# Three reorderings in a fused attention and two-layer MLP kernel: when a bank is copied out, through which buffers layer 1's sums leave, and when layer 2 begins

## The chip, the cores and the metric

The kernel runs on one core of one Trainium2 chip. The metric is the device time of one execution in microseconds (us). A run of the kernel gives one time; the profiler's trace comes from one further execution, which has a time of its own. The engines are TensorE (PE, with its weight loads listed as PEld), VectorE (DVE), ScalarE (ACT), GpSimd (POOL) and SyncE (SP, which here only issues DMAs). Each runs its own instructions strictly in the order in which they stand, and they meet through semaphores.

## What the reference computes

```python
# attention: 4 batches, 8 heads, 576 positions, head_dim 64
q_d, k_d, v_d = (t.reshape(B, H, 144, 4, D).mean(axis=3) for t in (q, k, v))
out_d = softmax(q_d @ k_d.T / 8) @ v_d                 # coarse: on means of 4 positions
local = softmax(where(|i - j| < 4, q @ k.T / 8, -1e9)) @ v
x = (repeat(out_d, 4) + local) as (2304, 512)          # 2304 tokens
# layer 1 (moe_w_in 512x2048, moe_w_out 2048x512)
h = x @ w_in; y = (h * sigmoid(1.702 * h)) @ w_out
# layer 2, the same weights again: g = h if h > 0 else exp(h) - 1
h2 = y @ w_in; out = elu(h2) @ w_out
```

The weights reach the kernel as 64-bit numbers and are converted on the chip, for each layer anew.

## The kernel before, in words

**Precision.** A float32 operand is split into a high and a low part (names ending in `h` and `l`); each product is the sum of three matmuls, high x high, low x high and high x low. So one step of 512 tokens (12 matmuls for four chunks of 128) costs the same on the way in (`h`) and out (`y` in layer 1, `o` in layer 2).

**Layer 1** goes over blocks of tokens (two of 256 that are later handled as one, `both`, then 512, 512, 512 and 256). For a block it takes the 2048 hidden columns in 16 steps `f`: 12 matmuls into a bank of PSUM (`h_part`), tanh on ACT (`h_tanh`), the gate on DVE (`h_gate`, which is what empties the bank), the high part on ACT (`h_high`) and the low part on DVE (`h_low`). Two steps later the result is multiplied with the outgoing weights into four banks `y` that stay open over the whole block (`y_part`). After the last step ACT copies the four banks to SBUF tiles `ye` (the line with `scale=0.5`), and SP writes them to a DRAM buffer, `ydram`. There are two banks for `h`; step f + 2 needs the bank of step f.

**Attention** of the later units (a unit is a batch and two heads) is interleaved with layer 1 in pieces: two matmul groups `qk` and `qkd` (local and coarse scores), exponentials on ACT, weights on DVE, transposes `pdt` and `ptr`, and the products with v, `pvd` and `pv`. Their results become x of a later block. All their PSUM tiles take turns in two banks of one pool (`spool`). In `turned_over` five transposes go out: four into one bank (`ptr0`), the fifth into the first columns of another (`ptr1`); DVE copies the first bank, ACT the second; then the coarse product goes into the remaining columns of the second bank. There are eight such units.

**Layer 2** reads `ydram` back (`load_y`), splits it (`split_y`: `x2h` on ACT, `x2l` on DVE) and runs the same scheme in `products_h2` and `products_o2`. Its weights are converted while layer 1's last block and layer 2's first block run: for each of 32 weight tiles ACT makes two passes (`ww2i`, `ww2o`, then `whl2i`, `whl2o`), DVE four. The conversion tiles `ww` of layer 1 lie in a pool `stage1`, three buffers deep.

**Order.** PE's order in this part is that of the code (`step1` writes it out). ACT, DVE and SP are ordered by a scheduler from the program order, the data and the buffers, with its own costs, so a change of buffers moves instructions there too. The lines that matter: `pt` and `turned_over`; in `y_part` the choice of the tile for `ye` (tag `g` of `gpool`, two buffers, which the gate's tiles use as well); in `step1` the call of `hidden2` for layer 2's steps 0 and 1, while layer 1's last two products are still to come.

Of the kernel before, what the change touches and what calls it, by code (L numbers as in the profile page):

```python
# [8 lines left out]
F32 = mybir.dt.float32  # L9
# [6 lines left out]
AF = mybir.ActivationFunctionType  # L16
# [3 lines left out]
P = 128  # L20
# [7 lines left out]
NK = 4  # L28
# [95 lines left out]
NPAIR = len(WINDOWS) // 2  # L124
# [9 lines left out]
def kernel(  # L134
# [20 lines left out]
    nc = tc.nc  # L155
# [3 lines left out]
    NBLK = len(BLOCKS1)  # L159
# [14 lines left out]
    for half in range(2):  # L174
        rows = slice(64 * half, 64 * half + 64)
        for a, e, lo in ((0, 1, -3), (1, 5, 0), (5, 6, 3)):
            m = mask[rows, a:e, :]
            for step, base, mult in ((1, -lo, -1), (-1, lo + 6, 1)):
                nc.gpsimd.affine_select(
                    out=m, in_=m, pattern=[[0, e - a], [step, KW]], compare_op=ALU.is_ge, fill=NEG,  # L180
# [182 lines left out]
    l1a = ExitStack()  # L363
# [46 lines left out]
    class Unit:  # L410
# [264 lines left out]
        def sums(self):  # L675
            return sumset[:, units.index(self) % NSUM]
# [45 lines left out]
        def pt(self, a, e):  # L722
            self.pt_copy(a, e, self.pt_piece(a, e))
# [204 lines left out]
    class Packed(Unit):  # L928
# [64 lines left out]
        def pt(self):  # L993
            while not self.weighed:
                deferred.pop(0)()
            self.PT = self.t([P, NPAIR, P], "PT")
            ps = self.ps([P, NPAIR - 1, P], "ptr0"), self.ps([P, P + SD], "ptr1")
            for i in range(NPAIR):
                nc.tensor.transpose(
                    out=ps[0][:, i] if i < NPAIR - 1 else ps[1][:, :P],  # L1000
                    in_=self.sl[:, 2 * i:2 * i + 2].rearrange("p s k -> p (s k)"), identity=ident,
                )
            nc.vector.tensor_copy(out=self.PT[:, :NPAIR - 1], in_=ps[0])
            nc.scalar.activation(out=self.PT[:, NPAIR - 1], in_=ps[1][:, :P], func=AF.Copy)
            return ps[1][:, P:]

        def pv_down_products(self, ps):
            for kc in range(2):
# [5 lines left out]
            return ps  # L1014

        def turned_over(self):
            ps = self.pt()
            self.pv_down_copy(self.pv_down_products(ps))

        def pv_products(self):  # L1020
            ps = [self.ps([P, 87, 4], f"pv{i}") for i in range(2)]
# [54 lines left out]
    queue = [(rest[NREST].turn, None, 1)]  # L1076
# [12 lines left out]
    nsplit = [0]  # L1089
# [118 lines left out]
    def sums_of(blk):  # L1208

        at = BOTH if blk in (0, 1) else blk  # L1210
        n = 512 if at == BOTH else BLOCKS1[at][1]
        if at not in yps:
            yps[at] = [
                ypool.tile([P, 512], F32, tag=f"y{i % 2}", name=f"y{i}_{at}") for i in range(NK * n // 512)
            ]
        first = 256 if blk == 1 else 0
        size = 512 if blk == BOTH else BLOCKS1[blk][1]
        per = 512 // n

        def sums(m):  # L1220
            at0 = first + n * (m % per)
            return yps[at][m // per][:, at0:at0 + size]

        return yps[at], per, sums

    def y_part(blk, fs, half):
        banks, per, sums = sums_of(blk)
        gh, gl = hg[blk, fs]
        opens = fs[0] == 0 and blk != 1
        last = fs[-1] == NF - 1  # L1230
        for m in (2 * half, 2 * half + 1):
            n = 0
            for i, f in enumerate(fs):
                for wp, gp in ((0, gh), (0, gl), (1, gh)):
                    nc.tensor.matmul(  # L1235
                        out=sums(m), lhsT=w_out(1, f, wp)[:, m, :], rhs=gp[:, i, :],
                        start=(opens and n == 0 and m % per == 0), stop=(last and n == 3 * len(fs) - 1),
                        skip_group_check=True,
                    )
                    n += 1  # L1240
            if last and m % per == per - 1:
                t0, tb = (0, 512) if blk == BOTH else BLOCKS1[blk]
                if blk == NBLK - 1:
                    t = x2pools[0].tile([P, 512], F32, tag="y32", name=f"ye{m // per}_{blk}", bufs=2)
                else:
                    t = gpool.tile([P, 512], F32, tag="g", name=f"ye{m // per}_{blk}", bufs=2)
                nc.scalar.activation(out=t, in_=banks[m // per], func=AF.Copy, scale=0.5)  # L1247
                nc.sync.dma_start(
                    out=ydram[m - per + 1:m + 1, :, t0:t0 + tb].rearrange("c p t -> p c t"),
                    in_=t.rearrange("p (a b) -> p a b", a=per),  # L1250
                )
        if half == 1:
            del hg[blk, fs]
# [11 lines left out]
    stage1 = ls1.enter_context(tc.tile_pool(name="stage1", bufs=1, side="right"))  # L1265
# [4 lines left out]
    wt1 = Weights(1, order1, stage1, 3, lambda tag: True, NSIGN)  # L1270
# [3 lines left out]
    kd, f = spare.pop(0)  # L1274
# [9 lines left out]
    steps = [(blk, fs) for blk in (0, 1) for fs in pairs[:FIRST]] + [(BOTH, (f,)) for f in range(2 * FIRST, NF)]  # L1284
# [94 lines left out]
    def hidden2(s):  # L1379
        bi, f = steps2[s]  # L1380
        wt2.need("i", f)
        low_part = products_h2(s)
        if bi + 1 < len(blocks):
            if 8 <= f < 8 + NK:
                load_y(bi + 1, f - 8)
            if 10 <= f < 10 + NK:
                split_y(bi + 1, f - 10)
        wt2.load(AHEAD + wt2.half - wt2.loaded)
        with behind():
            wt2.convert()  # L1390
        low_part()
        if s % 4 == 3:
            with behind():
                wt2.convert()
# [38 lines left out]
    def step1(si, blk, fs):  # L1433
        nonlocal prev, wt2, stage1, stage2, l1a, wextra, used
        chunks = []
        if blk is not None:
            last_blk = 1 if blk == BOTH else blk
            while not ready(last_blk):
                assert attend()
            if last_blk > 1 and fs[0] == 0:  # L1440

                with behind_step(si):
                    for _ in range(NK):
                        split_some(blk)
                while waiting:
                    prev = waiting.pop(0)
                    wt1.need("o", prev[1][-1])
                    chunks.append(products_y1(*prev))
            while nsplit[0] < NK * (last_blk + 1):
                split_some(last_blk)  # L1450
            wt1.need("i", fs[-1])
            chunks.append(products_h1(blk, fs))
            waiting.append((blk, fs))
            if blk == NBLK - 1:
                used |= {f"wi{f}" for f in fs}
        if len(waiting) > LAG or blk is None:
            prev = waiting.pop(0)
            wt1.need("o", prev[1][-1])
            chunks.append(products_y1(*prev))
        if blk is None:  # L1460
            hidden2(si - len(steps))
        nchunk = 0
        for chunk in chunks:
            for _ in chunk:
                if not wt1.finished() and (blk == 0 or si < 3 * FIRST and si % 2 == 1):
                    wt1.convert()
                with behind_step(si):
                    attend()
                if blk == 0:
                    split_some(1)  # L1470
                nchunk += 1
                if wt2 is not None and nchunk in (2, 3) and (nchunk == 2 or si % 2):
                    wt2.load(AHEAD + wt2.half - wt2.loaded)
                    with behind():
                        wt2.convert()
        if blk == NBLK - 1:
            f2 = fs[0] // 2
            if 1 <= f2 <= NK:
                load_y(0, f2 - 1)
            if 3 <= f2 < 3 + NK:  # L1480
                split_y(0, f2 - 3)
        if chunks and prev is not None and prev[0] == NBLK - 1:
            used |= {f"wo{f}" for f in prev[1]}
        if wt1.finished() and stage1 is not None:
            ls1.close()
            stage1 = None
        if not queue and nsplit[0] == NK * NBLK and l1a is not None:
            l1a.close()
            l1x.close()
            l1s.close()  # L1490
            hpools.append(ls2.enter_context(tc.tile_pool(name="hpool2", bufs=2, space=PSUM, side="right")))
            l1a = None
            stage2 = ls2.enter_context(tc.tile_pool(name="stage2", bufs=1, side="right"))
            x2pools.append(ls2.enter_context(tc.tile_pool(name="x2a", bufs=1, side="right")))
            wextra = ls2.enter_context(tc.tile_pool(name="wextra", bufs=1, side="right"))
            for i, tile2 in enumerate(order2):
                places[(2, *tile2)] = (wextra, f"we{i}") if i < NEXTRA else (wpool, released[i - NEXTRA])
            used |= {f"we{i}" for i in range(NEXTRA)}
            wt2 = Weights(2, order2, stage2, 3, lambda tag: tag in used, 0)
            wt2.load(AHEAD)  # L1500
# [14 lines left out]
    for s in range(LAG, len(steps2) + LAG):  # L1515
        if s < len(steps2):
            hidden2(s)
        f = steps2[s - LAG][1]
# [34 lines left out]
```

## Time and profile before

| | |
|---|---|
| median of 3 runs | 948.66 us (946.81 to 949.02) |
| the profiled execution, its own time | 949.08 us |
| its span (first to last instruction) | 947.3 us |
| PE busy | 921.0 us, 97% |
| DVE busy, ACT busy, POOL busy | 502.3 us, 465.4 us, 78.9 us |
| mean granted clock of TensorE | 0.998 |

The stretches, in us from the span's start: attention with layer 1's first blocks until about 180; layer 1's block 2 from there to about 303; block 3 to about 406; block 4 to about 494; the 256-token block 5 to about 546; layer 2 from about 535 to the end. PE's matmuls are pipelined, and their ends are modelled; what counts is where PE stands idle, and what ended each of these waits.

### The profile page before, as it was taken

How to read it: one execution, taken by the hardware profiler on the slowest of the kernel's cores; microseconds unless marked ns; L12 is line 12 of the kernel's file. 1: busy time of each engine (PE TensorE's matmuls, PEld its weight loads, DVE VectorE, ACT ScalarE, POOL GpSimd, SP SyncE). 2: the span in 40 equal slices, each digit the busy share in tenths (PEclk: the TensorE clock that was granted, in tenths of full speed). 3: DMA queues.
4: the chain of work that ended last, by engine and by line, in shares of the span. 5: the costliest groups of instructions: out<-in, count | busy, mean ns of one | idle time of the engine just before them, and what ended most of it. 6: DMA issues, size and time to landing. Idle time of an engine off the chain costs nothing. (4 is left out here: it accounts for less than half of the span.)

```text
span 947.3 us, 14840 instructions
## 1 busy us (share of the span) xinstructions
PE 921.0 (97%) x5812; PEld 756.0 (80%) x5812; DVE 502.3 (53%) x920; ACT 465.4 (49%) x1131; POOL 78.9 (8%) x126
## 2 busy tenths in 40 slices
PE   8998999989999899999999989999999999999998
PEld 5687888767777678888889978877888888888897
DVE  6999987665665542322227898773224222322232
ACT  6879997454353532232235576653334333433343
POOL 3615114101111100000000000000000000000000
PEclk9999999999999999999999999999999999999999
DMA  9897803333332104010029620011002000100010
GB/s 186 185 254 227 226 21 67 87 66 62 64 62 70 45 15 134 0 45 1 1 69 351 248 80 9 1 45 45 0 1 79 1 1 0 56 1 1 1 45 23
DMA packets 113590, 68.04 MB, mean 72 GB/s; under 512 B 81008, under 2 KB 103024, under 8 KB 113520
## 3 DMA queue, kind: packets, MB, share of 16 engines
q1 hardware_dynamic: 111152, 66.50, 25.9%
q8 instruction: 46, 0.75, 0.4%
q10 hardware_dynamic: 2368, 0.59, 0.4%
q14 instruction: 24, 0.20, 0.1%
HBM read 57.63 MB, written 9.44 MB: 71 GB/s over the span
## 5 line engine op out<-in xcount | busy, mean ns | idle before, releaser
L1407 PE MATMUL o<-whl2o,g2h 128*128 128x512 f32 x576 | 181.3, 395 | 3.1 <-ACT ye L1247 2.8
L1358 PE MATMUL h<-x2h,whl2i 128*128 128x512 f32 (+1 forms) x640 | 159.0, 370 | 0.0
L1235 PE MATMUL y<-g1h,whl1o 128*128 128x512 f32 (+1 forms) x512 | 153.5, 367 | 0.0
L1168 PE MATMUL h<-xh,whl1i 128*128 128x512 f32 (+1 forms) x640 | 145.1, 351 | 2.7 <-DVE g L1181 2.7
L1368 DVE SCALAR_TENSOR_TENSOR g<-e,h 128x512 f32<-128x512 f32 (+1 forms) x80 | 50.7, 634 | 177.9 <-ACT e L1366 177.6
L1358 PEld LDWEIGHTS h<-x2h,whl2i 128*128 128x128 f32 x640 | 114.3, 188 | 22.4
L1407 PEld LDWEIGHTS o<-whl2o,g2h 128*128 128x128 f32 x576 | 107.5, 189 | 27.9 <-ACT ye L1247 3.2
L1365 ACT ACTIVATE e<-h 128x512 f32<-128x512 f32 (+1 forms) x80 | 44.3, 554 | 159.5 <-PE h L1358 159.5
L1168 PEld LDWEIGHTS h<-xh,whl1i 128*128 128x128 f32 x640 | 106.1, 189 | 20.3 <-DVE g L1181 3.5
L1407 PE MATMUL o<-whl2o,g2l 128*128 128x512 f32 x288 | 113.0, 392 | 0.0
L1181 DVE SCALAR_TENSOR_TENSOR g<-g,h 128x512 f32<-128x512 f32 x64 | 43.9, 686 | 122.1 <-ACT g L1177 122.1
L1235 PEld LDWEIGHTS y<-g1h,whl1o 128*128 128x128 f32 x512 | 92.6, 189 | 16.7 <-issue 1.4
L1177 ACT ACTIVATE g<-h 128x512 f32<-128x512 f32 x64 | 38.1, 595 | 123.1 <-PE h L1168 118.2
L1235 PE MATMUL y<-g1l,whl1o 128*128 128x512 f32 (+1 forms) x256 | 93.0, 363 | 0.0
L1358 PE MATMUL h<-x2l,whl2i 128*128 128x512 f32 (+1 forms) x320 | 79.6, 370 | 0.0
L1168 PE MATMUL h<-xl,whl1i 128*128 128x512 f32 (+1 forms) x320 | 75.9, 351 | 0.0
L1375 DVE TENSOR_TENSOR g2l<-g,g2h 128x512 fp32r<-128x512 f32 (+1 forms) x80 | 51.6, 646 | 36.8 <-ACT g2h L1373 21.6
L1373 ACT ACTIVATE g2h<-g 128x512 fp32r<-128x512 f32 (+1 forms) x80 | 47.1, 589 | 42.8 <-DVE g L1368 42.7
L1358 PEld LDWEIGHTS h<-x2l,whl2i 128*128 128x128 f32 x320 | 56.7, 188 | 11.0
L1407 PEld LDWEIGHTS o<-whl2o,g2l 128*128 128x128 f32 x288 | 54.5, 189 | 12.1
L1168 PEld LDWEIGHTS h<-xl,whl1i 128*128 128x128 f32 x320 | 53.3, 189 | 8.5 <-issue 0.8
L1194 DVE TENSOR_TENSOR g1l<-g,g1h 128x512 fp32r<-128x512 f32 x64 | 44.4, 693 | 25.4 <-ACT g1h L1187 25.1
(142 smaller groups left out, 1289.6 us busy)
## 6 DMA issues: line engine op xcount, KB each, us to landing
wst1i<-in_moe_w_in_dram SPq DMA_DIRECT2D x16, 512.0 KB
wst1o<-in_moe_w_out_dram SPq DMA_DIRECT2D x16, 512.0 KB
wst2i<-in_moe_w_in_dram SPq DMA_DIRECT2D x16, 512.0 KB
wst2o<-in_moe_w_out_dram SPq DMA_DIRECT2D x16, 512.0 KB
vr<-in_v_dram SPq DMA_DIRECT2D x32, 144.0 KB
out_dram<-ot SPq DMA_DIRECT2D x18, 256.0 KB
y<-ydram SPq DMA_DIRECT2D x16, 256.0 KB
ydram<-ye SPq DMA_DIRECT2D x14, 256.0 KB
```

The lines of the kernel that those rows point to most:

```text
L1168: nc.tensor.matmul(out=hps[blk, fs][:, i, :], lhsT=w_in(1, f, c, wp), rhs=columns(xp, c), start=(n == 0), stop=(n >= len(todo) - nf), skip ...
L1177: return nc.scalar.activation(out=g, in_=hps[blk, fs], func=AF.Tanh, scale=0.851)
L1181: return nc.vector.scalar_tensor_tensor(out=g, in0=g, scalar=1.0, in1=ph, op0=ALU.add, op1=ALU.mult)
L1194: return nc.vector.tensor_tensor(out=gl, in0=g, in1=gh.bitcast(F32), op=ALU.subtract)
L1235: nc.tensor.matmul(out=sums(m), lhsT=w_out(1, f, wp)[:, m, :], rhs=gp[:, i, :], start=(opens and n == 0 and m % per == 0), stop=(last and ...
L1358: nc.tensor.matmul(out=ph[:, :n], lhsT=w_in(2, f, c, wp), rhs=xp[:, c, :n], start=(i == 0), stop=(i == 3 * NK - 1),)
L1365: nc.scalar.activation(out=e[:, :n], in_=ph[:, :n], func=AF.Relu, scale=-1.0)
L1368: urgent["dve"] = nc.vector.scalar_tensor_tensor(out=g[:, :n], in0=e[:, :n], scalar=-1.0, in1=ph[:, :n], op0=ALU.add, op1=ALU.max)
L1373: nc.scalar.activation(out=gh[:, :n], in_=g[:, :n], func=AF.Copy)
L1375: return lambda: nc.vector.tensor_tensor(out=gl[:, :n], in0=g[:, :n], in1=gh[:, :n].bitcast(F32), op=ALU.subtract)
L1407: nc.tensor.matmul(out=ops[bi][i], lhsT=gp[:, i * P:(i + 1) * P], rhs=wo[wp], start=(f == 0 and m == 0), stop=(f == NF - 1 and m == 2),)
```

## The change

First, in `pt` the fifth transpose is asked for ahead of the other four, and `turned_over` now asks for the coarse product before the two copies. Second, the `ye` tiles of all blocks but the last are taken from `stage1` (tag `ww`, three buffers); that pool is closed later. Third, in `step1` the call of `hidden2` stands behind layer 1's products of the same step.

```diff
@@ pt
-            for i in range(NPAIR):
+            for i in (NPAIR - 1, *range(NPAIR - 1)):
                 nc.tensor.transpose(...)
-            nc.vector.tensor_copy(out=self.PT[:, :NPAIR - 1], in_=ps[0])
-            nc.scalar.activation(out=self.PT[:, NPAIR - 1], in_=ps[1][:, :P], func=AF.Copy)
-            return ps[1][:, P:]
+            return ps
@@ turned_over
-            ps = self.pt()
-            self.pv_down_copy(self.pv_down_products(ps))
+            first, second = self.pt()
+            down = self.pv_down_products(second[:, P:])
+            nc.vector.tensor_copy(out=self.PT[:, :NPAIR - 1], in_=first)
+            nc.scalar.activation(out=self.PT[:, NPAIR - 1], in_=second[:, :P], func=AF.Copy)
+            self.pv_down_copy(down)
@@ y_part
+                elif stage1 is not None:
+                    t = stage1.tile([P, NK * P], F32, tag="ww", name=f"ye{m // per}_{blk}", bufs=3)
                 else:
                     t = gpool.tile([P, 512], F32, tag="g", name=f"ye{m // per}_{blk}", bufs=2)
@@ step1
-        if blk is None:
-            hidden2(si - len(steps))
         nchunk = 0
         for chunk in chunks:
...
+        if blk is None:
+            hidden2(si - len(steps))
         if blk == NBLK - 1:
...
-        if wt1.finished() and stage1 is not None:
+        if not queue and nsplit[0] == NK * NBLK and l1a is not None:
             ls1.close()
             stage1 = None
-        if not queue and nsplit[0] == NK * NBLK and l1a is not None:
             l1a.close()
```

PE, the first of the eight units in block 2, before (`ptr_2_0_0` are the two banks, `sl` the local weights, `pdT` and `vd` the coarse product's operands):

```order
L999 MATMUL ptr_2_0_0_2958<-ident,sl_0_0_2659 128x128 x4
L999 MATMUL ptr_2_0_0_2959<-ident,sl_0_0_2659 128x128
L1010 MATMUL ptr_2_0_0_2959<-pdT_0_0_2932,vd_0_0_2404 64x144 x4
L1168 MATMUL h_2_4_2984<-xh_2619,whl1i_852 128x512 x4
L1168 MATMUL h_2_4_2984<-xl_2620,whl1i_852 128x512 x4
```

and now:

```order
L999 MATMUL ptr_2_0_0_2958<-ident,sl_0_0_2659 128x128
L999 MATMUL ptr_2_0_0_2957<-ident,sl_0_0_2659 128x128 x4
L1008 MATMUL ptr_2_0_0_2958<-pdT_0_0_2931,vd_0_0_2404 64x144 x4
L1169 MATMUL h_2_4_2983<-xh_2619,whl1i_852 128x512 x4
L1169 MATMUL h_2_4_2983<-xl_2620,whl1i_852 128x512 x4
```

The transpose into the bank that the coarse product shares has come to the front; the product keeps its place on PE, but no copy stands between it and the transposes any more.

DVE at the start of block 2, before (`g_2_0` and `g_2_1` are the gates of steps 0 and 1, `qT_1_0` and `kT_1_0` the turned q and k of the next attention unit, `sumset`, `pd`, `sl` the weights of the present one):

```order
L640 TENSOR_SCALAR nmd_0_0_2712<-nmd_0_0_2712 72x4
L558 STREAM_TRANSPOSE qT_1_0_2738<-rawq_1_0_2643 128x576
L548 TENSOR_REDUCE qd_1_0_2742<-qT_1_0_2738 128x144
L558 STREAM_TRANSPOSE kT_1_0_2740<-rawk_1_0_2648 128x576
L548 TENSOR_REDUCE kd_1_0_2744<-kT_1_0_2740 128x144
L1181 SCALAR_TENSOR_TENSOR g_2_0_2762<-g_2_0_2762,h_2_0_2727 128x512
L1194 TENSOR_TENSOR g1l_0_2767<-g_2_0_2762,g1h_0_2765 128x512
```

and now:

```order
L640 TENSOR_SCALAR nmd_0_0_2712<-nmd_0_0_2712 72x4
L1182 SCALAR_TENSOR_TENSOR g_2_0_2762<-g_2_0_2762,h_2_0_2727 128x512
L558 STREAM_TRANSPOSE qT_1_0_2738<-rawq_1_0_2643 128x576
L548 TENSOR_REDUCE qd_1_0_2742<-qT_1_0_2738 128x144
L1195 TENSOR_TENSOR g1l_0_2767<-g_2_0_2762,g1h_0_2765 128x512
L687 TENSOR_SCALAR sumset<-sumset 128x14
L688 RECIPROCAL sumset<-sumset 128x14
L1182 SCALAR_TENSOR_TENSOR g_2_1_2792<-g_2_1_2792,h_2_1_2772 128x512
L691 TENSOR_TENSOR pd_0_0_2713<-pd_0_0_2713,sumset 72x576
L691 TENSOR_TENSOR sl_0_0_2659<-sl_0_0_2659,sumset 128x640
L1195 TENSOR_TENSOR g1l_1_2797<-g_2_1_2792,g1h_1_2795 128x512
L558 STREAM_TRANSPOSE kT_1_0_2740<-rawk_1_0_2648 128x576
```

`kT_1_0` has moved from ahead of gate 0 to behind the low part of step 1. On PE nothing has moved here: the `qk` products that read `kT_1_0` stand in the middle of step 2 (`h_2_2`) in both kernels.

PE where layer 2 starts, before (`y_5` are layer 1's last sums, `h_0` to `h_2` and `o_0` layer 2's first steps):

```order
L1235 MATMUL y_5_5581<-g1l_14_5936,whl1o_2475 128x256
L1235 MATMUL y_5_5581<-g1h_14_5934,whl1o_2475 128x256
L1358 MATMUL h_2_6132<-x2h_5686,whl2i_5663 128x512 x4
L1358 MATMUL h_2_6132<-x2l_5687,whl2i_5663 128x512 x4
L1358 MATMUL h_2_6132<-x2h_5686,whl2i_5663 128x512 x4
L1407 MATMUL o_0_6164<-whl2o_5793,g2h_6000 128x512 x2
```

and now:

```order
L1361 MATMUL h_1_6088<-x2l_5687,whl2i_5641 128x512 x4
L1361 MATMUL h_1_6088<-x2h_5686,whl2i_5641 128x512 x4
L1361 MATMUL h_2_6132<-x2h_5686,whl2i_5663 128x512 x4
L1361 MATMUL h_2_6132<-x2l_5687,whl2i_5663 128x512 x4
L1361 MATMUL h_2_6132<-x2h_5686,whl2i_5663 128x512 x4
L1410 MATMUL o_0_6164<-whl2o_5793,g2h_6034 128x512 x2
```

Between the last `y_5` and `o_0` there was one step of layer 2, and now there are two; `h_0` stands where `h_1` stood.

## Rows read from the trace of the kernel before

**Rows 1.** Waits of PE: us in total, times, longest us.

```profile
PE ptr L1010 <- ACT PT L1004: 4.0, 8, 0.8
PE o L1407 <- ACT ye L1247: 2.8, 1, 2.8
PE h L1168 <- DVE g L1181: 2.7, 3, 1.6
```

**Rows 2.** Timeline of PE: start us, us, instructions [idle before <-releaser]; the transposes.

```profile
171.02 0.60 PE L730 MATMUL ptr<-ident,sl 128*70 128x128 f32 x4
171.38 0.48 PE L1235 MATMUL y_both<-g1h_both,whl1o 128*128 128x512 f32 x1
...
206.68 0.71 PE L999 MATMUL ptr<-ident,sl 128*128 128x128 f32 x5
207.84 0.71 PE L1010 MATMUL ptr<-pdT,vd 72*64 72x144 f32 x8 [0.46 <-ACT PT L1004]
208.48 1.19 PE L1168 MATMUL h<-xh,whl1i 128*128 128x512 f32 x4
```

**Rows 3.** Timeline of PE at the start of block 2.

```profile
191.51 1.19 PE L1168 MATMUL h<-xh,whl1i 128*128 128x512 f32 x4 [1.60 <-DVE g L1181]
...
193.11 0.81 PE L962 MATMUL qk<-kT,qT 64*64 64x64 f32 x40
...
197.85 0.68 PE L628 MATMUL qkd<-kd,qd 64*72 64x144 f32 x4 [0.33 <-DVE sl L976]
...
203.57 0.45 PE L712 MATMUL pdt<-ident,pd 72*72 72x72 f32 x4 [0.28 <-ACT pd L656]
```

**Rows 4.** Timelines of ACT, DVE and SP at the same place.

```profile
190.14 0.60 ACT L1177 ACTIVATE g<-h 128x512 f32<-128x512 f32 x1 [1.39 <-DMA ydram<-ye_both]
...
187.06 0.78 DVE L558 STREAM_TRANSPOSE kT<-rawk 128x576 f32<-128x576 f32 x1 [0.19 <-DMA rawk<-in_k_dram]
...
193.28 0.17 DVE L687 TENSOR_SCALAR sumset<-sumset 128x14 f32<-128x14 f32 x1 [0.30 <-ACT sl L649]
...
195.17 0.68 DVE L1181 SCALAR_TENSOR_TENSOR g<-g,h 128x512 f32<-128x512 f32 x1
...
189.15 1.69 SPq L459 DMA_DIRECT2D rawq<-in_q_dram  x3
```

**Rows 5.** Windows: stretch, length, busy us of each engine, then PEclk, DMA share, GB/s.

```profile
191.50:195.00 3.50, 3.48 (x51) 2.69 (x52) 2.35 (x5) 2.23 (x10) 0.00 (x0) 1.00 0.68 109
...
551.50:554.30 2.80, 2.76 (x7) 2.18 (x8) 2.77 (x5) 1.86 (x4) 0.00 (x0) 0.51 0.64 199
554.30:556.00 1.70, 1.70 (x8) 1.38 (x7) 1.60 (x4) 1.26 (x3) 0.00 (x0) 0.81 0.58 163
```

**Rows 6.** Timelines of PE and ACT where block 3 begins.

```profile
311.42 1.19 PE L1168 MATMUL h<-xh,whl1i 128*128 128x512 f32 x4 [0.79 <-DVE g L1181]
...
315.30 0.77 PE L999 MATMUL ptr<-ident,sl 128*128 128x128 f32 x5 [0.86 <-ACT pdT L720]
316.84 0.71 PE L1010 MATMUL ptr<-pdT,vd 72*64 72x144 f32 x8 [0.78 <-ACT PT L1004]
...
307.31 1.21 ACT L1247 ACTIVATE ye<-y 128x512 f32<-128x512 f32 x2 [5.20 <-DMA ydram<-ye]
...
314.85 0.69 ACT L720 ACTIVATE pdT<-pdt 72x288 f32<-72x288 f32 x2
```

**Rows 7.** Timeline of PE where block 5 begins.

```profile
499.99 0.74 PE L1168 MATMUL h<-xh,whl1i 128*128 128x256 f32 x4 [0.33 <-DVE g L1181]
```

**Rows 8.** Timelines of PE and ACT where layer 2's first outgoing product begins.

```profile
551.54 1.22 PE L1407 MATMUL o<-whl2o,g2h 128*128 128x512 f32 x2 [2.78 <-ACT ye L1247]
...
550.91 0.58 ACT L1247 ACTIVATE ye<-y 128x512 f32<-128x512 f32 x1
```

**Rows 9.** DVE in layer 2's first block: a window, and one gate.

```profile
555.00:565.00 10.00, 10.00 (x45) 8.14 (x45) 9.69 (x18) 7.82 (x14) 0.00 (x0) 1.00 0.25 72
...
582.41 0.69 DVE L1368 SCALAR_TENSOR_TENSOR g<-e,h 128x512 f32<-128x512 f32 x1 [1.71 <-ACT e L1366]
```

## Prediction

> **What bounds the kernel now.** The page first: PE is busy for 97% of the span, and its slices are full from attention's end to the last output. So the kernel ends when PE has got through its list, and a change is worth the PE idle time that it removes or adds. The second view is therefore the list of PE's waits [rows 1]; the reader is to see how short it is, and that three entries in it carry 9.5 us: the coarse product waits eight times for the copy of the fifth transpose (4.0), layer 2's first `o` product once for an eviction `ye` (2.8), and the `h` products three times for a gate (2.7). These are the three things that the change touches. Third, PE's timeline at each of these places, with ACT and DVE beside it, to see what would be late next; and the windows, for the granted clock behind a wait.
>
> **The eight coarse products.** At the first one five transposes start at 206.68, the product at 207.84 and the next step at 208.48 [rows 2]. Four transposes elsewhere take 0.36 us from start to the next group's start [rows 2], so five take 0.45 to 0.5. With no copy in between the product starts at about 207.16, 0.68 earlier. The idle time shown, 0.46, is less, because the modelled end of the last transpose hides part of it; 0.46 and 0.71 are the bounds. Seven places at 0.68 give 4.8 us (3.2 to 5.0); the eighth is taken with block 3 below. What is added: ACT's copy now waits for the product (0.64 us, 207.84 to 208.48), and the next reader of that copy, `pv`, comes at least one step of 2.7 us later. DVE's copy has its four transposes one transpose (0.09) later. And the first transpose now needs the bank that the second `pdT` copy frees, not the first; that matters only where ACT is late, in block 3.
>
> **Block 2's start.** Today the third step stands 1.60 us for gate 0 [rows 3], because ACT's tanh waited 1.39 for the DRAM write of an eviction whose buffer is a gate's [rows 4]. With `ye` in other buffers the tanh no longer waits. But the scheduler then moves `kT_1_0` on DVE behind gate 0, gate 1 and both low parts, and PE needs it in the middle of the third step. Without its wait that step starts at 191.51 - 1.60 = 189.91. Six of its matmuls took 1.60 (191.51 to 193.11, the restart in it), so PE is at `qk` at 191.5, and a full step takes about 2.75: step 0 ended at 189.91 - 2.75 = 187.2. Tanh 0.60, so gate 0 starts on DVE at 187.8. Ahead of `kT_1_0` then stand two gates and two low parts (0.60 to 0.69 each: 2.4 to 2.8), `qT` and `qd` (0.7 to 0.78 each: 1.4 to 1.6), and `sumset`, its reciprocal and the two weightings, 195.17 - 193.28 = 1.89 for the four [rows 4]. Sum 5.7 to 6.2, so `kT_1_0` starts at 193.5 to 194.0 and is done, 0.78 later, at 194.3 to 194.8. Today it ran at 187.06 and cost PE nothing. So PE reaches `qk` 1.6 us earlier and then stands for 2.9 to 3.3; the products start at about 194.6, 1.5 later than now. Two short waits behind (0.33 and 0.28 idle [rows 3]) then lose their cause, since PE is later and DVE and ACT are not: at the ratio of the transposes (0.46 idle for 0.68 lost) about 0.9 to 1.2 back. Net 0.3 to 0.6 us lost; I take 0.4, with -0.8 and +1.0 as bounds.
>
> To this comes the clock. After the 2.78 us wait of `o` [rows 8] the granted clock was 0.51 for 2.8 us and 0.81 for 1.7 us [rows 5], the lower of the two levels (1.2 GHz) and then a mixture: 2.8 x 0.49 + 1.7 x 0.19 = 1.7 us lost. After the 1.60 us wait here it stayed at 1.00 [rows 5]. The new wait is longer than the one that lowered the clock, so I count 1.7 us (bounds 0 and 1.7). This place together: 2.1 us lost.
>
> The Trainium skill says in "TensorE: Matmul & The Clock Gate", section "Part 1: The HAM clock gate", that half rate is the array's default and only activity releases it, so that an idle stretch brings the low clock back. By that rule the new wait here is paid twice, as counted; without it the sum would be 1.7 us lower. The trace agrees at 551.5 (0.51) and shows no fall after 1.60 us.
>
> SP: the next unit's `rawq` loads (at 189.15 now [rows 4]) stand in its queue behind the fourth eviction, which ACT now does behind step 1's high part, at about 193. They are read by DVE about 200 and later, some 7 us behind; no cost. The fourth `y` bank is needed by step 0's outgoing product, more than 4 us later.
>
> **Block 3's start.** Here ACT stood 5.20 us for the write of an eviction until 307.31 [rows 6], and PE later 0.79 for gate 0, 0.86 for `pdT` and 0.78 for the copy. The third eviction no longer waits and the fourth goes behind seven exponentials, so ACT's coarse exponentials and tanh start some 1.5 us earlier; the 0.79 goes. But ahead of the `pdT` copies now stand that eviction (0.6) and a high part (0.6): of the 1.5 us about 0.4 is left, so the second copy, which ended at 314.85 + 0.69 = 315.54, ends at about 315.1. PE arrives 0.8 earlier and waits for it: the transposes start at about 315.2 instead of 315.30. Then the pair shrinks from 316.84 - 315.30 = 1.54 to 0.48. Together 1.2 us gained (0.4 to 1.9).
>
> **Block 5's start.** The wait of 0.33 for a gate [rows 7] goes, 0.5 us with the refill (0.3 to 0.5). Between blocks 3 and 4 PE did not wait, so nothing is to be had there.
>
> **Layer 2's start.** `o` begins at 551.54 after 2.78 us idle [rows 8], so layer 1's last product ended one step (2.75) before 548.8, at 546.0, and the second eviction began only at 550.91, 4.9 later: ACT had weight conversions ahead of it that wait for a DVE with hardly a gap. Now two steps of layer 2 lie between, so the last `y` ends at 543.2. With the same lag the eviction ends at 543.2 + 4.9 + 0.6 = 548.7, just when PE arrives. The wait goes, and the slow clock behind it with it: 2.8 + 1.7 = 4.5 us (2.5 to 4.8). Late next: DVE. In 555 to 565 it is busy for 9.69 of 10 us [rows 9], and its list is as long as before while PE is 4.5 us earlier. The first `o` steps then have little margin on the low parts (I find near none for step 1, over 2 us for the others). DVE catches up afterwards: by 582.41 it waits 1.71 us for the exponential in a step [rows 9].
>
> **The sum.** -4.8 + 2.1 - 1.2 - 0.5 - 4.5 = -8.9 us. The profiled execution took 949.08, so 940.2; it lay 0.42 above the median of the runs shown, so I predict 939.8.
>
> **The rivals.**
>
> *The clock stays up in block 2.* The estimate of the wait there, 2.9 to 3.3, lies close to the 2.78 that lowered it, and only one such fall is on record. Then 1.7 us less: 938.1.
>
> *DVE takes over behind layer 2's start.* For it: 9.69 of 10 us; the eviction has no margin by the sum above. Against: the wait there only has to be reached by 548.7, and DVE has idle time from about 575. A wait of the size that is now removed would come back at step 0 or 1, below the length at which the clock fell: +2.8, 942.6.
>
> *The product still waits for the copy.* Both use one bank, and if the changed order still put the copy's release ahead, the eight pairs would stay: 939.8 + 4.8 + 1.1 = 945.7. Against it: in the changed order the product stands behind the transposes alone.
>
> *Slower: the weights run out.* One mechanism: layer 2's 32 weight tiles are converted by a DVE at its limit, and they are done when they are done. If that were fixed in time, whatever PE gains before would be waited for again during layer 2's first block (8.9 us back), and two waits as long as the one that lowered the clock would add 2 x 1.7: 949.1 + 3.4 = 952.5, 952.1 against the median. It decides if DVE has no idle time left between the start of layer 2 and the last tile. Against: the 1.71 us gap [rows 9] shows DVE paced by PE for several steps.
>
> **Chances.** Forecast 0.50, with a range of its own from 938.8 to 941.5; clock stays up 0.22; DVE takes over 0.17; product still waits 0.05; slower 0.06. What a measurement of this kernel can tell from no change is about 0.3%, 2.8 us: faster is below 945.8, slower above 951.5. The first three are faster, the fourth is at the edge, and of the last most lies above: faster 0.89, same 0.06, slower 0.05. The range for 8 in 10 takes in the first three and their bounds: 936.5 to 943.5.
>
> **What would show it.** Right: no wait of `ptr` for the ACT copy in PE's list, and some 1.1 us from the transposes to the next step; a wait of `qk` for DVE `kT` near 191.5, of about 3 us, with a granted clock near 0.5 behind it; no `h` wait for a gate at blocks 2, 3 and 5; the transposes of block 3 still behind `pdT`; no wait of `o` for `ye`, and a clock of 1.00 there. Wrong: a `qk` wait under 2 us or well over 4; `o` waiting for `ye`, for a low part or for `whl2o` by more than a microsecond; or new waits between 575 and 640.

## The result, and the profile after

The changed kernel takes 938.53 us (median of 4 runs, 937.30 to 939.82) against 947.81 before (4 runs); the ratio is 0.9902, with a 95% interval of 0.988 to 0.9923. In a later comparison it was 938.38 against 946.32, ratio 0.9917 (0.9897 to 0.9937). The prediction was 939.8. Where the text below says how many us less a kernel takes than the kernel before, it goes by the ratio, which is not exactly the quotient of the two medians.

PE's list of waits in the changed kernel (us in total, times, longest) begins so:

```profile
PE qk L962 <- DVE kT L558: 3.8, 2, 3.2
...
PE ptr L999 <- ACT pdT L720: 1.2, 1, 1.2
```

None of the three entries of [rows 1] is left. What is new is a wait of `qk` for `kT`, 3.16 of the 3.8 us at one place (the rest is in the opening), and the wait of the transposes for `pdT` has grown from 0.86 [rows 6] to 1.20.

PE's timeline at the places of the change (start, length, instructions, idle before):

```profile
189.87 0.61 PE L1169 MATMUL h<-xl,whl1i 128*128 128x512 f32 x2
193.64 0.97 PE L962 MATMUL qk<-kT,qT 64*64 64x64 f32 x40 [3.16 <-DVE kT L558]
...
207.07 0.71 PE L999 MATMUL ptr<-ident,sl 128*128 128x128 f32 x5
207.71 0.71 PE L1008 MATMUL ptr<-pdT,vd 72*64 72x144 f32 x8
208.35 0.50 PE L1169 MATMUL h<-xh,whl1i 128*128 128x512 f32 x1
...
312.41 0.95 PE L999 MATMUL ptr<-ident,sl 128*128 128x128 f32 x5 [1.20 <-ACT pdT L720]
313.29 0.71 PE L1008 MATMUL ptr<-pdT,vd 72*64 72x144 f32 x8
...
543.37 0.39 PE L1410 MATMUL o<-whl2o,g2h 128*128 128x512 f32 x1
```

From the transposes to the step behind the coarse product it is now 208.35 - 207.07 = 1.28 us, where it was 208.48 - 206.68 = 1.80 [rows 2]; at `o` no idle time is shown. Behind layer 2's start one wait above 0.15 us is left, 0.37 for `whl2o` at 615; before it was 0.33, at 625.

DVE's timeline where block 2 begins, in the same columns:

```profile
187.13 0.69 DVE L1182 SCALAR_TENSOR_TENSOR g<-g,h 128x512 f32<-128x512 f32 x1 [2.63 <-ACT g L1178]
187.73 0.77 DVE L558 STREAM_TRANSPOSE qT<-rawq 128x576 f32<-128x576 f32 x1
...
190.16 0.63 DVE L1182 SCALAR_TENSOR_TENSOR g<-g,h 128x512 f32<-128x512 f32 x1
...
192.12 0.68 DVE L1195 TENSOR_TENSOR g1l<-g,g1h 128x512 fp32r<-128x512 f32 x1
192.72 0.77 DVE L558 STREAM_TRANSPOSE kT<-rawk 128x576 f32<-128x576 f32 x1
```

DVE stands 2.63 us for the tanh and then works without a gap through both gates and both low parts before it turns `kT`. ACT's timeline where layer 2's `o` begins:

```profile
537.62 0.62 ACT L252 ACTIVATE whl2o<-ww2o 128x512 fp32r<-128x512 f32 x1
538.14 0.58 ACT L1250 ACTIVATE ye<-y 128x512 f32<-128x512 f32 x1
...
539.70 0.59 ACT L1250 ACTIVATE ye<-y 128x512 f32<-128x512 f32 x1
```

The last eviction ends at 540.29, 3.1 us before `o` needs the bank.

Windows of the changed kernel (length, busy us of the engines, then the granted clock):

```profile
191.40:194.20 2.80, 0.56 (x36) 0.59 (x40) 2.77 (x5) 0.55 (x2) 0.00 (x0) 0.99 0.43 121
194.20:197.00 2.80, 2.80 (x25) 2.20 (x16) 1.91 (x6) 0.00 (x0) 0.00 (x0) 0.50 0.81 130
197.00:199.00 2.00, 2.00 (x10) 1.37 (x10) 0.69 (x1) 1.44 (x7) 0.00 (x0) 0.86 0.31 51
...
550.00:555.00 5.00, 5.00 (x23) 4.09 (x23) 5.00 (x10) 3.58 (x7) 0.00 (x0) 1.00 0.28 81
555.00:565.00 10.00, 10.00 (x45) 8.12 (x44) 9.86 (x17) 7.40 (x14) 0.00 (x0) 1.00 0.14 40
```

The half-rate stretch has moved from behind `o` (0.51 in [rows 5]) to behind `qk`. DVE is busy for 9.86 us of 10 behind layer 2's start, and PE stands for nothing there.

Where the time went shows in the distance between marks on PE's timeline, in us. The marks: the first `h` of block 2; the first and the eighth group of five transposes; the first `o`; the last `o`. Each column is a start minus a start in the kernel's profile; the experiments' kernels stand here too, with their medians (before was 946.3 to 946.8 in their comparisons):

| kernel | h to ptr 1 | ptr 1 to 8 | ptr 8 to o | o to end | median, us |
|---|---|---|---|---|---|
| before | 22.50 | 141.25 | 203.61 | 391.74 | 947.81 |
| changed | 23.68 | 136.76 | 199.54 | 390.13 | 938.53 |
| changed, again | 22.14 | 136.78 | 199.54 | 390.09 | 938.38 |
| product first alone | 22.78 | 138.04 | 202.95 | 390.18 | 942.43 |
| results first alone | 22.67 | 141.19 | 201.24 | 390.15 | 944.68 |
| other buffers alone | 24.88 | 140.25 | 201.43 | 390.26 | 944.96 |
| without other buffers | 22.61 | 137.88 | 200.18 | 390.08 | 939.14 |
| kT first | 20.91 | 136.79 | 199.54 | 390.09 | 935.86 |
| kT in the middle | 21.10 | 136.78 | 199.54 | 390.09 | 936.04 |
| transposes twice | 23.67 | 140.55 | 200.09 | 390.15 | 943.54 |
| kT first, old order | 20.93 | 136.47 | 199.54 | 390.12 | 935.65 |
| buffers and kT first | 20.92 | 140.04 | 201.38 | 390.23 | 941.90 |

In the two profiles of the comparison the columns differ by +1.18, -4.49, -4.07 and -1.61, together -9.0 us. These two executions took 949.08 and 939.30, 9.8 us apart; the remaining 0.8 lies in the opening, whose length differs from execution to execution: block 2's first `h` came between 182.0 and 184.2 us in these twelve profiles.

### The profile page after: what moved, and what is told of

Its sections match the earlier page's. It is cut to its first block, busy times and chain, and to the rows that moved or that the text cites. A ratio compares the mean times of both kernels' runs of the same rounds, so it can differ in the third digit from the quotient of the medians.

```text
span 937.5 us, 14829 instructions
## 1 busy us (share of the span) xinstructions
PE 919.5 (98%) x5812; PEld 756.0 (81%) x5812; DVE 502.2 (54%) x920; ACT 464.9 (50%) x1131; POOL 76.6 (8%) x126
## 4 chain that ended last, share of the span: by engine, by line
PE 85%; DVE 8%; ACT 3%; DMA 2%; SPq 1%; issue 1%; ACTq 0%; DVEq 0%
PE o L1410 21%; PE h L1361 21%; PE y L1236 16%; PE h L1169 15%; PE y_both L1236 3%; PE h_both L1169 2%; DVE wst1i L230 1%; SPq L473 1%; DMA wst1i<-in_moe_w_in_dram 1%; PE qkd L628 1%; DVE wst1o L230 1%; PE pv L1035 1%; ACT sl L649 1%; ACT pd L656 1%; PE qk L962 1%; DMA vr<-in_v_dram 1%
```

## The experiments

**The parts alone.** Product first:

```diff
-            for i in range(NPAIR):
+            for i in (NPAIR - 1, *range(NPAIR - 1)):
...
-            ps = self.pt()
-            self.pv_down_copy(self.pv_down_products(ps))
+            first, second = self.pt()
+            down = self.pv_down_products(second[:, P:])
...
```

> The kernel before with the first part alone: the coarse product is asked for ahead of the two copies, the evictions and the order at layer 2 as before. If each of the eight places gives what the changed kernel's trace shows at two of them (1.28 us from the transposes to the next step in place of 1.80 and 1.81), seven give 7 x 0.53 = 3.7 us, and the one in block 3, where the shrinking stretch was 1.54 us, up to 0.9: 4.2 to 4.6 us less. By my prediction's own price (0.68 each) it would be 4.8 + 0.9 = 5.7. Rival: the time that PE gains at these places is waited for later (for pv's copy, or for the gates of a block), then under 1.5 us. Shown by: no wait of ptr for the ACT copy in PE's list, and the waits of h for a gate still there at three places.

942.43 us against 946.58, ratio 0.9956 (0.9939 to 0.9973): 4.2 us less. The eight stretches are 1.28 at six places, 1.41 at one and 1.52 (from 2.18) in block 3; the eight differences sum to 4.2. Two lines of its list of PE's waits:

```profile
PE h L1169 <- DVE g L1182: 4.2, 3, 1.9
PE o L1408 <- ACT ye L1248: 2.1, 1, 2.1
```

The waits for the gates grew from 2.7 to 4.2 us, so part of the gain is handed back there; the wait for `ye` shrank by 0.7. That the time fell by just as much as the eight places is therefore in part luck: the first three columns of the table are 3.6 lower, and the rest fits the clock (a mean of 0.9987 in these six runs for 0.9976 before, see below).

Results first:

```diff
-        if blk is None:
-            hidden2(si - len(steps))
         nchunk = 0
...
+        if blk is None:
+            hidden2(si - len(steps))
         if blk == NBLK - 1:
```

> The kernel before with the third part alone: the last two groups of y products stand ahead of layer 2's first two steps. If the wait of o for the eviction (2.78 us) and the half-rate stretch behind it (1.7 us) both go, 4.5 us less. Rival 1: the clock's fall was not the wait's doing, or cost nothing: 2.8 us less. Rival 2: DVE, busy for 9.7 of 10 us behind it, takes the gain back: 0 to 1.7 less, with a new wait of o or h between 540 and 575.

944.68 us, ratio 0.9973 (0.9959 to 0.9986): 2.6 us less, below the 4.5 of my theory. In its profile the wait is gone and `o` waits for nothing else, and the last two columns of the table are 2.4 and 1.6 lower. What fell short is the clock: the 1.6 was lost in the profiled execution of before, but not in each (below). The time alone fits rival 1 (2.8 less) as well; against it speak the clocks of the runs (a mean of 0.9987 for 0.9976).

Other buffers:

```diff
+                elif stage1 is not None:
+                    t = stage1.tile([P, NK * P], F32, tag="ww", name=f"ye{m // per}_{blk}", bufs=3)
...
-        if wt1.finished() and stage1 is not None:
-            ls1.close()
-            stage1 = None
...
```

> The kernel before with the second part alone: the evictions of all blocks but the last leave through the conversion buffers. My theory: a loss of about 1.2 us at block 2 (a wait of qk for kT of about 3 us and a half-rate stretch behind it, in place of the 1.60 us wait for the gate), a gain of 0.8 to 1.2 at block 3 (the 0.79 wait goes, the wait for pdT grows) and 0.5 at block 5: from -0.5 to +0.8 us, no difference that can be measured. Rival: the evictions' buffers were what cost the time, and all three waits of h for a gate (2.7 us) go with nothing in their place: 2.7 us less.

944.96 us, ratio 0.9983 (0.9971 to 0.9994): 1.6 us less (0.6 to 2.7), between my theory (0.5 at best) and the rival (2.7). Block 2 lost 2.4 in its profile, as foreseen and more, and the stretch with block 3 gained 1.0; what I had missed is the 2.2 in the third column. The gate's wait in block 5 is gone, and the wait of `o` for `ye` is 1.17 us in place of 2.78, without the third part. The second eviction starts 0.78 earlier than before (550.13 for 550.91 [rows 8]) while layer 2's first `h` starts 0.85 later: the conversions ahead of it do not keep step with PE. Why they run earlier I did not find out.

Without the other buffers (the changed kernel, with this line of its diff undone and the pool closed where it was):

```diff
-                elif stage1 is not None:
-                    t = stage1.tile([P, NK * P], F32, tag="ww", name=f"ye{m // per}_{blk}", bufs=3)
...
```

> The changed kernel without its second part: product first, results first, the evictions through the gate buffers as before. If the parts add up, this is the sum of the first and the third part alone, 4.4 + 4.5 = 8.9 us less than before, the same as the whole change within 1 us, since the second part then gives next to nothing. Rival: the second part is needed for the others, because ACT stands behind the evictions' writes: then 7 us or less.

939.14 us, ratio 0.9926 (0.991 to 0.9941): 7.0 us less. By its number alone that is the rival's (7 us or less); but it is also the sum of the first and third part as measured (4.2 + 2.6), so these two add up and do not need the second. What was too much is 8.9. In the profiles the four columns are 8.4 lower, and 1.6 of that is the half-rate stretch, which not each execution of before has.

**The clock.** The changed kernel a second time:

> The changed kernel itself, for comparison on the same chip: 0.990 of the kernel before, about 9.3 us less, with the wait of qk for kT of about 3.2 us and a granted clock near 0.50 behind it.

Ratio 0.9917. The wait is there to the hundredth, and the clock does not fall. PE's timeline:

```profile
192.94 0.81 PE L962 MATMUL qk<-kT,qT 64*64 64x64 f32 x40 [3.16 <-DVE kT L558]
```

The windows of the wait and of the work behind it, with a granted clock of 1.00 in both:

```profile
190.00:192.80 2.80, 0.00 (x0) 0.00 (x0) 2.80 (x5) 1.11 (x2) 0.00 (x0) 1.00 0.25 86
192.80:195.60 2.80, 2.65 (x48) 2.31 (x49) 2.52 (x6) 0.17 (x1) 0.00 (x0) 1.00 0.80 135
```

In the profile of the other buffers alone, the same wait is followed by a longer fall, as its windows from the wait's end on show:

```profile
194.40:197.00 2.60, 2.53 (x43) 2.25 (x44) 1.82 (x6) 0.00 (x0) 0.00 (x0) 0.50 0.79 130
197.00:199.00 2.00, 2.00 (x6) 1.52 (x6) 0.73 (x1) 0.23 (x1) 0.00 (x0) 0.50 0.63 104
199.00:201.00 2.00, 2.00 (x8) 1.30 (x8) 0.69 (x1) 2.00 (x9) 0.00 (x0) 0.60 0.01 1
```

So a wait of 3.16 us cost 0, 1.5 or 2.7 us beside itself (22.14, 23.68 and 24.88 in the first column). The fall is a chance, not a fixed price: of the ten timed executions of the changed kernel three show a mean granted clock of 1.00 and seven 0.996 to 0.998.

`kT` in the middle, ahead of the second step's gate alone (in `h_gate`; `turned_k` is the unit's transpose that writes `kT`, and `issue_after` puts the gate behind it in DVE's order):

```diff
-        return nc.vector.scalar_tensor_tensor(out=g, in0=g, scalar=1.0, in1=ph, op0=ALU.add, op1=ALU.mult)
+        with ExitStack() as stack:
+            if (blk, fs[0]) == (2, 1):
+                stack.enter_context(tc.issue_after(rest[NREST + 1].turned_k.ins))
+            return nc.vector.scalar_tensor_tensor(out=g, in0=g, scalar=1.0, in1=ph, op0=ALU.add, op1=ALU.mult)
```

> The changed kernel with kT_1_0 ahead of the gate of block 2's second step alone: it stands two instructions of DVE earlier (a gate and a low part, 1.2 us), so the wait of qk shrinks from 3.16 to about 1.9 us. It lies between the 1.60 us after which the clock stayed at 1.00 and the 2.78 us after which it fell. If the clock falls here too: 1.2 us less than the changed kernel, with a window near 0.50 behind the wait. If it stays up: 1.2 + 1.7 = 2.9 us less. If the clock costs nothing: 1.2 less, whatever the windows show.

936.04 us, ratio 0.9889 (0.9871 to 0.9907), 2.3 less than the changed kernel on the same chip. The wait is shorter and the clock stays up. PE's timeline:

```profile
192.48 0.81 PE L962 MATMUL qk<-kT,qT 64*64 64x64 f32 x40 [2.13 <-DVE kT L558]
```

The window behind the wait:

```profile
192.40:195.00 2.60, 2.52 (x48) 2.17 (x49) 2.56 (x6) 0.65 (x2) 0.00 (x0) 1.00 0.81 131
```

The wait is 1.0 us shorter, not 1.2, and the first column is 1.0 lower than in the changed kernel's second profile (21.10 for 22.14); the other 1.3 of the 2.3 us is the clock. The timed executions say so too: those with a granted clock of 1.00 differ by 1.0 only (a median of 937.07 in three of the changed kernel, of 936.0 in four here), and the changed kernel's three others, at 0.996 and 0.997, took 938.82 to 940.47. That the clock costs nothing is out.

**`kT` first.** The changed kernel with both gates held behind it, the same edit with another condition:

```diff
+        with ExitStack() as stack:
+            if blk == 2 and fs[0] <= 1:
+                stack.enter_context(tc.issue_after(rest[NREST + 1].turned_k.ins))
...
```

> The changed kernel with kT_1_0 held ahead of the gates of block 2's first two steps on DVE. If the second part's loss is the order on DVE, then neither the 1.60 us wait of before nor the 3.16 us wait of the changed kernel is there, the clock stays at 1.00, and the two short waits (0.33 and 0.28) stay gone or come back by less than 0.6 in all: 3 to 3.5 us less than the changed kernel, some 12.5 less than before. Rival: the step that now starts earlier runs into the next late thing (the low parts, which now stand behind kT, or the gate of step 1): then the time is that of the changed kernel within 1 us, with a new wait of h or y near 191 to 198.

935.86 us (935.25 to 936.34), ratio 0.9887 (0.9869 to 0.9905): 10.7 less than before, 2.5 less than the changed kernel, not the 3 to 3.5 expected. PE's timeline shows why:

```profile
189.23 0.81 PE L962 MATMUL qk<-kT,qT 64*64 64x64 f32 x40
...
193.67 1.14 PE L628 MATMUL qkd<-kd,qd 64*72 64x144 f32 x8 [0.68 <-DVE sl L976]
...
199.30 0.44 PE L712 MATMUL pdt<-ident,pd 72*72 72x72 f32 x4 [0.19 <-ACT pd L656]
```

Neither long wait is there, and short ones stand behind it: the rival in part. It is faster than both kernels of the comparison all the same. From `qk` to the transposes PE takes 13.89 us here, 13.57 before and 11.89 in the changed kernel's second profile. So the first column gains only 1.2 us on that profile (20.91 for 22.14); the rest of the 2.5 fits the clock, as with `kT` in the middle.

**The transposes' price.**

```diff
-            for i in (NPAIR - 1, *range(NPAIR - 1)):
+            for i in (NPAIR - 1, *range(NPAIR - 1)) * 2:
```

> The changed kernel with the five transposes ahead of each coarse product done twice into the same bank. My prediction priced five of them at 0.48 us (from a row of four narrower ones, 0.09 each), and the changed kernel's trace shows 0.64 from the first to the product. If a transpose is dearer than I took it, the ten take 1.28 until the product starts, 5.1 us more in all. If 0.09 is right and a fixed 0.16 us comes from elsewhere (the change from one kind of product to the other), the ten take 1.1, 3.7 us more in all.

943.54 us in one run, 4.2 more than the changed kernel's profiled execution (939.30), whose first column is the same within 0.01. PE's timeline at the first place:

```profile
206.94 1.25 PE L999 MATMUL ptr<-ident,sl 128*128 128x128 f32 x10
208.12 0.71 PE L1008 MATMUL ptr<-pdT,vd 72*64 72x144 f32 x8
```

Ten take 1.18 until the product, five 0.64: five more cost 0.54, and 0.10 is fixed. The second column is 3.8 higher, seven times 0.54. Neither theory has it quite; a transpose costs 0.11 here, not 0.09, and a small step is left over.

**The order of the transposes.** `kT` first, with the fifth transpose last again:

```diff
-            for i in (NPAIR - 1, *range(NPAIR - 1)):
+            for i in range(NPAIR):
```

> The kernel with kT_1_0 held ahead of the two gates, and the five transposes in the order of before (the fifth last). My prediction said that the fifth transpose first matters only where ACT is late, in block 3: there PE waits 1.2 us for the second pdT copy. With the old order the four transposes into the first bank need only the first copy (0.35 us earlier), so the product comes 0.3 to 0.4 us earlier at that one place, and at the seven others the stretch stays 1.28: 0.3 less in the trace, no difference in the times. Rival: the fifth first is what lets the product start early; then the seven stretches grow above 1.28.

935.65 us (934.91 to 936.25), ratio 0.9884 (0.9867 to 0.9901), not to be told from the fifth first. In block 3, on PE's timeline:

```profile
309.36 0.77 PE L999 MATMUL ptr<-ident,sl 128*128 128x128 f32 x5 [1.20 <-ACT pdT L720]
310.05 0.71 PE L1008 MATMUL ptr<-pdT,vd 72*64 72x144 f32 x8
```

0.69 to the product for 0.88: 0.19 of the expected 0.3 to 0.4, and another 0.12 at the third place. The second column is 0.3 lower. The gain comes from the product ahead of the copies alone.

The expectation had one thing the wrong way round: the transposes do not start earlier with the old order, they wait 1.20 us for `pdT` in both. In the changed kernel ACT's two `pdT` copies overlap:

```profile
311.94 0.71 ACT L720 ACTIVATE pdT<-pdt 72x288 f32<-72x288 f32 x2
```

By their single spans in the trace the first ends at 312.36 and the second at 312.65. The fifth transpose starts at 312.41 and the next at 312.70, 0.05 us behind each. With the old order the first of the four starts at 309.36, 0.05 behind its first copy (309.31). So in both orders the transpose that is asked for first gets the bank that the first copy frees. With the fifth first it is the other four that stand for the second copy, and this is what the old order saves.

**Buffers and `kT` first**, the two edits shown above together, on the kernel before:

> The kernel before with the second part alone, and kT_1_0 held ahead of the gates of block 2's first two steps. In the second part alone, from block 2's first h to its first transposes PE took 24.88 us (the 3.16 us wait and 6 us below full clock behind it); before it took 22.50, and in the changed kernel with kT first 20.91. If the loss is the order on DVE and the clock behind its wait, this kernel takes 20.9 there, so it gains 1.6 us on before, plus the 1.0 between the transposes and the 2.2 from the last transposes to the first o product that the second part alone showed: 4.8 us less than before, 3 less than the second part alone. Rival: the second part's buffers give nothing by themselves: within 2 us of before.

941.90 us against 946.76, ratio 0.9953 (0.9938 to 0.9969): 4.5 us less. 20.92 in the first column, as foreseen. Alone the second part is worth some 4.5 us, of which its order on DVE takes back 3, the clock's fall included. On top of the other two parts it gives less, 10.7 - 7.0 = 3.7 us (`kT` first against the kernel without the other buffers), as the third part already takes away the wait of `o`.

## Why the prediction came out as it did

The forecast held, in sum and in most of its places: no wait for the copy, a wait of `qk` for `kT` inside the 2.9 to 3.3 foreseen, half rate behind it in the profiled execution, no wait for a gate at the three places, no wait of `o` for `ye`. As a difference it was -8.9 us, and the two comparisons gave -9.3 and -7.9. As a time, 938.53 lies 0.3 below the forecast's own range (938.8 to 941.5), since the kernel before came out at 947.81 in the comparison and not at 948.66. Several sizes were off, and that they nearly cancel is luck.

**The product: 0.68 was 0.53.** The step that failed is "five take 0.45 to 0.5". I had priced them by four narrower ones [rows 2]; doubled, they cost 0.54, with 0.10 fixed. The bounds (0.46 and 0.71) held at six of the seven places; the third, where the four transposes stand for the second `pdT` copy, gave 0.40. The seven lost 1.2 us against the forecast.

**Block 2's wait: +0.4 was -0.4.** The wait itself came as worked out, and `qk` started 1.3 us later after block 2's first `h` than before (10.25 for 8.93). The step that failed is the refund: I gave the two short waits (0.33 and 0.28 idle [rows 3]) 0.9 to 1.2 us back, and it was 1.68, the 13.57 - 11.89 from above. The idle time shown before a group was not even half of what the group came late.

**The clock.** I charged 1.7 us at block 2 and credited 1.7 at layer 2, each in full from one fall in one execution. In the profiles of the comparison that came out so (23.68 - 22.14 = 1.5 and 391.74 - 390.13 = 1.6), by luck; the runs tell it as a mean. The granted clock of each timed execution, averaged: 0.9976 before (45 runs), 0.9977 changed (10), 0.9987 with results first alone (12), 0.9995 in the three changed kernels with `kT` moved (15). By these I estimate that the wait of `o` cost some 0.0011 x 945 = 1.0 us and the wait of `qk` 0.0018 x 938 = 1.7, each uncertain by about half a microsecond by the scatter of the runs. (Buffers and `kT` first, with no wait above 1.2 us behind its opening, shows 0.9987 in six runs: so few runs say little.) My rival "the clock stays up" is thus no other course of the kernel but some of its executions.

The Trainium skill says in "TensorE: Matmul & The Clock Gate", section "Part 1: The HAM clock gate", that the watch on the array's activity runs free of the program. That would fit a fall after one wait and none after the same wait in another execution; no run here shows the cause.

**Blocks 3 and 5, layer 2.** Block 3 was forecast at 1.2: the second column fell by 4.49, of which the five ordinary places before it and the one behind have 3.05, so 1.4. Its two terms were both off: the transposes start some 0.8 us earlier, not 0.1, and the pair shrinks by 0.66 (1.54 to 0.88), not by 1.06. That the first transpose would need the second copy's bank was wrong, as shown above. The third column was forecast at 0.68 + 0.5 + 2.8 = 4.0 and fell by 4.07. Its working was wrong in one step, "with the same lag": the eviction ended 2.4 us after the last `y`, not 5.5, so the margin was 3.1 us and not none. ACT's order is why. Before, two weight passes (the first of them late), two exponentials and a third pass behind a 0.46 us wait stood between the last `y` (545.87) and the first eviction:

```profile
546.01 0.68 ACT L227 ACTIVATE ww2o<-wst2o 128x512 f32<-128x512 f32 x1 [1.72 <-DVE whl2i L256]
...
548.82 0.63 ACT L252 ACTIVATE whl2i<-ww2i 128x512 fp32r<-128x512 f32 x1 [0.46 <-DVE ww2i L245]
549.35 0.58 ACT L1247 ACTIVATE ye<-y 128x512 f32<-128x512 f32 x1
```

In the changed kernel one pass, begun at 537.62, is all that the first eviction (538.14) finds ahead of it when the last `y` is through at 537.91. And I gave the wait of `o` wholly to the third part; the second alone takes 1.6 of it.

**The rivals.** DVE did not take over, although it is as full as I feared (9.86 of 10): the last column is 390.1 to 390.3 in each kernel but the one before. With it falls the slower rival, weights that are done when they are done. The price that I gave to DVE's taking over was too low by its own premise: a wait of 2.8 us would have been as long as the one that lowered the clock, not shorter.

The mean clock is the same in both kernels (0.9976 and 0.9977, a difference of 0.1 us): the wait of `qk` costs about what the wait of `o` (1.0) and the rest (0.9987 against 0.9995, 0.8) gave back. The sum is then -0.36 - 4.49 - 4.07 - 0.1 = -9.0 us, which lies in the intervals of both comparisons (7.3 to 11.4 and 6.0 to 9.7 us less).

## What to carry to other kernels

A change of buffers moves more than the waits for them: read from the new order what the scheduler moves on the other engines, since mending one DVE instruction's place was worth 2.5 us of the 10.7 in the end, about half of it clock. Price a removed wait from start to start of the groups around it, and a new operation by a row of its own shape. What one profile shows of the clock is one throw; take its price from the clocks of many executions.

## What the runs showed of the hardware

A long idle stretch of PE is followed by a lower granted clock in some executions only, and the loss differs. In these twelve profiles, waits of 1.60 to 2.13 us inside layer 1 and at layer 2's start (six of them) were followed by no fall; of the one of 2.78 and four of 3.16, four were, with a cost of 1.5 to 2.7 us. In the opening a fall stood behind a wait of 1.29 us for `qd` in two of the twelve profiles (which all have that wait), and behind one of 1.39 for `vd` in one. The start of the fall is not tied to the end of the wait: with the other buffers alone the granted clock was already 0.50 in the last part of the wait (193.80 to 194.40), and in the changed kernel's first profile it was still 1.00 while `qk` had begun (193.64 to 194.10). Timed executions of the kernel before that differ in the mean clock differ in time: the median is 945.18 us at 0.999 and above (10 runs), 946.57 at 0.997 to 0.998 (20) and 948.40 at 0.996 and below (15). Without the long wait the spread goes too: 935.25 to 936.34 over five runs with `kT` first.
